# Moving the next unit's row preparation behind the output products in a linear-attention and mixture-of-experts kernel on one Trainium2 core

## The chip, the cores and the metric

The kernel runs on one core of a Trainium2 chip. The metric is the device time of one execution, in microseconds, and the value that counts is the median of several executions. A core has TensorE (in the profile PE for matmuls and PEld for loading the stationary operand), VectorE (DVE), ScalarE (ACT), GpSimd (POOL) and the queue engine SyncE (SP). The engines run side by side; each works through its own queue in order, and an instruction waits on semaphores for what other engines and the DMA transfers have done.

## What is computed

```python
x = A_x                                       # 2048 rows of 512
h = x + _A_ref(_layernorm(x), wqkv, w_phi, wo)  # linear attention, 32 heads
h2 = h + _B_ref(_layernorm(h), w_gate, w1, w2)  # 8 experts, one per row
# inside _B_ref, D=512, F=1792, E=8:
logits = xf @ w_gate
topk_idx = jnp.argsort(-logits, axis=-1)[:, :1]
for e in range(E):
    out = out + w * (_silu(xf @ w1[e]) @ w2[e])   # w: the gate where row picks e, else 0
```

All of it is in float32.

## The kernel before, in words

**Two parts.** The first part, up to about 300 us, computes the attention, writes h with its normalisation factors and gate into the buffer `hbuf` in device memory, and sorts the rows by their expert. The second part runs the experts, and the change is in it. Its rows are worked off in units of 128 rows, `unit(u)`. Here units 0 to 10 run first, then two wide stages of 288 rows (`wide(0)`, `wide(1)`), then units 11 and 12; later units are skipped by a test on the chip. `POS` is 11, so `POS - 1` is unit 10, which also prepares the wide stage.

**Products in two halves.** A float32 product is made of three fast ones: each operand is split into a high part (ACT writes it, `hi_of`, L76) and a low part (DVE subtracts, `lo_of`, L79), and `mm3` adds high x high, high x low and low x high (L82 to L84). The weights of an expert come in seven chunks of 1 MB (`raw`), each split in two pieces of 128x1024 into `whi` and `wlo`. Chunks 0, 1, 2 and the first half of chunk 3 hold the first weight matrix; the second half of chunk 3 holds the weights of output products 0 and 1, chunk 4 those of products 2 to 5, chunk 5 of 6 to 9, chunk 6 of 10 to 13.

**One unit.** `gather(u + 1)` fetches the rows of the next unit with an indirect DMA on POOL (`rows`, L145) into one of two row buffers `xg`; it must wait until the scatter of unit u - 1 has read that buffer. `gemm1` makes the hidden values in four column chunks (PSUM tile `mh`), ACT applies silu (L183, tile `hs`), PE transposes each chunk (`tr`, L209, PSUM tile `mtr`), and ACT and DVE split the transposed values (`hA` for chunks 0 and 1, `hThi` and `hTlo` for 2 and 3; the last one is half as wide, 128x256). `g2` makes fourteen output products into PSUM tile `my`, three matmuls each. DVE scales them by the gate and adds h (before: L1077), and POOL scatters the rows to the output (`scatter`, L152).

**Preparing the next rows.** `prework(u + 1)` normalises the gathered rows (ACT L161 for units 1 and 2, DVE L163 after that; tile `xn`), lets PE transpose them (L166, four transposes into another `mtr` bank), and splits the result into `xhi` and `xlo`, which the next unit's `gemm1` reads. The trace shows some of these tiles under other names that share their memory (`xwh`, `xwl`). The `mtr` and `mh` tiles share four PSUM banks in turn. In unit 10, `tile0` does the same for the three tiles of the wide stage's 288 rows (DVE L893, PE L897).

**Splitting the next expert's weights.** `split(u, c)` (L884) does its work only if a flag computed on the chip says that unit u begins with another expert; `fetch` (L880, L881) then reloads `raw[c]` on SP. In this data units 4 to 7 and unit 9 are full of such splits.

**What sets the order.** The code is written in one sequence, and a scheduler puts each engine's instructions in an order of its own: what is ready first by its reckoning goes first, with the sequence of the code as priority. `after(i)` adds an order edge: what the block issues on i's engine stands behind i in that engine's queue, without a wait for its end. The order is fixed when the program is built, and an instruction that waits holds up all that stands behind it on its engine.

In the code before, `prework(u + 1)` stands ahead of the output products:

```python
load_flags(u + 1)
if u != POS:
    with after(si if u < 3 else None):
        prework(u + 1)
g2(py, 0, 2)
tr(3)
```

Of the kernel before, what the change touches and what calls it, by code (L numbers as in the profile page):

```python
# [15 lines left out]
OP = mybir.AluOpType  # L16
# [6 lines left out]
S, D, H, DH = 2048, 512, 32, 16  # L23
F, E = 1792, 8
NJ = 14
# [6 lines left out]
POS = 11  # L32
# [3 lines left out]
WC = 24  # L36
# [12 lines left out]
def kernel(  # L49
# [28 lines left out]
    def lo_of(dst, src, hi):  # L78
        return V.tensor_tensor(dst, src, hi.bitcast(F32), op=OP.subtract)  # L79
# [64 lines left out]
    def rows(dst, col, n=P):  # L144
        G.indirect_dma_start(out=dst[0:n, :], out_offset=None, in_=hbuf if col else hbuf[0:S // 2, :],  # L145
                             in_offset=bass.IndirectOffsetOnAxis(ap=gidx[0:n, col:col + 1], axis=0))
# [4 lines left out]
    def scatter(src, col, n=P):  # L151
        G.indirect_dma_start(out=out, out_offset=bass.IndirectOffsetOnAxis(ap=sidx[0:n, col:col + 1], axis=0),  # L152
                             in_=src[0:n, 0:D], in_offset=None, bounds_check=S - 1, oob_is_err=False)
# [4 lines left out]
    def prework(u, pool=None):  # L158
        g = xg[u % 2]
        if u < 3:  # L160
            A.activation(xn2[0][:, 0:D], g[:, 0:D], AF.Identity, bias=g[:, D:D + 1], scale=g[:, D + 1:D + 2])  # L161
        else:
            V.tensor_scalar(xn2[0][:, 0:D], g[:, 0:D], g[:, D + 1:D + 2], g[:, D:D + 1], op0=OP.mult, op1=OP.add)  # L163
        pt = pool.tile([P, 512], F32, name="mtx", tag="s") if pool else bank("mtr")
        for k in range(KD):
            T.transpose(pt[:, k * P:(k + 1) * P], xn2[0][:, k * P:(k + 1) * P], ident)  # L166
        ptv = pt.rearrange("p (k t) -> p k t", k=KD)
        h = hi_of(xhi[par(u)], ptv)
        return h, lo_of(xlo[par(u)], ptv, xhi[par(u)])

    pin = {}
# [28 lines left out]
    def split_chunk(c):  # L200
        for i in range(2):
            hi_piece(c, i)
            lo_piece(c, i)

    def tr(c, hTf=None):
        fw = FC[c]
        pt = bank("mtr")
        for j in range(fw // P):
            T.transpose(pt[:, j * P:(j + 1) * P], hs[c % 2][:, j * P:(j + 1) * P], ident)  # L209
        ptv = pt[:, 0:fw].rearrange("p (k t) -> p k t", t=P)  # L210
        n = JF - 4 * c if hTf is not None else fw // P
        if n > 0:
            hi_of(hThi[c][:, 0:n, :], ptv[:, 0:n, :])
            lo_of(hTlo[c][:, 0:n, :], ptv[:, 0:n, :], hThi[c][:, 0:n, :])
        if hTf is not None:
            n = max(n, 0)
            return hi_of(hTf[:, 4 * c + n - JF:4 * c + fw // P - JF, :], ptv[:, n:, :])
# [25 lines left out]
    def after(i):  # L243
        return tc.issue_after(i.ins) if i is not None else ExitStack()
# [638 lines left out]
    def split(u, c):  # L883
        with tc.If(flags[u][0] > 0):  # L884
            split_chunk(c)
        fetch(u, c)

    def load(c, e):
        nc.sync.dma_start(raw[c], w12_at(e, c))
# [10 lines left out]
    def tile0(t, src):  # L900
        o, n = WT[t]
        ptv = tile3(t, src, None)
        hi_of(xW[0][:, :, o:o + n], ptv)
        return lo_of(xW[1][:, :, o:o + n], ptv, xW[0][:, :, o:o + n])
# [44 lines left out]
    def wide_out(w, t, r):  # L949
# [4 lines left out]
        V.scalar_tensor_tensor(r[0:n, 0:D], pt[0:n, :], r[0:n, D + 2:D + 3], r[0:n, 0:D], op0=OP.mult, op1=OP.add)  # L954
        scatter(r, WC + 3 * w + t, n)

    def unit(u):
        def g2(py, j0, j1):
            for j in range(j0, j1):
                c, jj = divmod(j, 4)  # L960
                m = mm3(py, hThi[c][:, jj, :], hTlo[c][:, jj, :], w2_at(whi, j), w2_at(wlo, j),
                        j == 0, j == NJ - 1)
            return m

        def g2p(py, w, j0, j1):
            for j in range(j0, j1):
                c, jj = divmod(j, 4)
                m = T.matmul(py, hThi[c][:, jj, :], w2_at(w, j), start=w is whi and j == 0,
                             stop=w is wlo and j == JF - 1)
                if w is whi:  # L970
                    m = T.matmul(py, hTlo[c][:, jj, :], w2_at(w, j), start=False, stop=False)
            return m

        if u:
            if u == POS - 1:
                rows(xg[0], WC + 1)
                rows(xg[1], WC)
            elif u + 1 < NU and u != POS:
                gather(u + 1)
            for c in range(4):  # L980
                si = silu(c, gemm1(u, c))
                if c:
                    tr(c - 1)
                if u == 1 and c == 0:
                    with after(pin["g1"]), after(pin["y"]):
                        wide_rows()
                if u == POS:
                    if c < 2:
                        if c == 0:
                            split_chunk(3)  # L990
                            fetch(u, 3)
                            wide_out(1, 0, xr[0])
                            gather(u + 1)
                        wide_out(1, c + 1, xr[c + 1])
                        if c:
                            load(6, e11)
                elif c < 3:
                    split(u, 4 + c)
        else:
            tr(2, hTf())  # L1000
            h3 = tr(3, hTf())
        py = pss.tile([P, 512], F32, name="my", tag="s")
        if u == 0:
            with after(g2p(py, whi, 0, 2)):
                gm, sidx_ = index(scratch, lambda: g2p(py, whi, 2, 4))
            with after(gm):
                gm = g2p(py, whi, 4, JF)
            def plain(j0, j1):
                for j in range(j0, j1):
                    m = T.matmul(py, hTf()[:, j - JF, :], w2_at(raw, j), start=False, stop=False)  # L1010
                return m

            with after(gm):
                m = plain(JF, NJ)
            with after(sidx_), after(m):
                last, ft, fc = flags_of(scratch)
            with after(last), after(ft):
                lo_piece(3, 1)
                lo4 = split_lo(4)
                m = g2p(py, wlo, 0, 2)  # L1020
            with after(h3), after(lo4), after(m):
                xh, xl = prework(1)
            g2p(py, wlo, 2, JF)
            with after(xh), after(xl):
                load_fl(0, 8)
            load_flags(0)
            load_flags(1)
            ew0, ew1 = [nc.values_load(ewi[0:1, i:i + 1], engines=[ENG.SP], min_val=0, max_val=E - 1)
                        for i in range(2)]
            e11_ = nc.values_load(flg[96:97, POS:POS + 1], engines=[ENG.SP], min_val=0, max_val=E - 1)  # L1030
            we.extend((ew0, ew1, e11_))
            for c in range(4):
                fetch(0, c)
                split(1, c)
            with after(xh), after(xl):
                for c in (5, 6):
                    split_hi(c)
                    split_lo(c)
            V.tensor_copy(utot, endx[:, EV:EV + 1])
            for c in range(4, NW):  # L1040
                fetch(0, c)
        elif u == POS - 1:
            tile0(1, xg[0])
            rows(xg[0], WC + 2)
            tile0(0, xg[1])
            rows(xg[1], u)
            g2(py, 0, 2)
            tr(3)
            for c in range(4):
                split_chunk(c)  # L1050
                load(c, we[1])
            with after(g2(py, 2, 9)):
                tile0(2, xg[0])
            g2(py, 9, NJ)
        else:
            if u + 1 < NU:
                if u == 5:
                    load_fl(8, POS)
                if u == POS:
                    load_fl(NF, NU)  # L1060
                load_flags(u + 1)
                if u != POS:
                    with after(si if u < 3 else None):
                        prework(u + 1)
            g2(py, 0, 2)
            tr(3)
            if u == POS:
                prework(u + 1)
                split_chunk(6)
                fetch(u, 6)  # L1070
            if u + 1 < NU:
                for c in range(4):
                    split(u + 1, c)
            g2(py, 2, NJ)
        g = xg[u % 2 if u != POS - 1 else 1]
        with after(xl if u == 0 else None):
            pin["y"] = V.scalar_tensor_tensor(g[:, 0:D], py, g[:, D + 2:D + 3], g[:, 0:D], op0=OP.mult, op1=OP.add)  # L1077
        scatter(g, u)

    we = []  # L1080
    for u in range(POS):
# [94 lines left out]
```

## Time and profile before

| | |
|---|---|
| median of 3 runs | 744.52 us (741.51 to 744.82) |
| the profiled execution's own time | 743.65 us |
| its span, first to last instruction | 742.0 us |
| PE busy | 681.6 us (92%) |
| DVE busy | 475.3 us (64%) |
| ACT busy | 356.1 us (48%) |
| POOL busy | 186.6 us (25%) |
| mean granted TensorE clock | 0.965 |

The profile is one execution seen by the hardware profiler. The page gives the busy time of each engine and the costliest groups of instructions. The trace behind it answers finer questions: the table of stretches gives the busy time of each engine between two moments; the waits list who waited for whom; the timeline of an engine lists its instructions with start, length, engine, line, what is written from what, how many, and in square brackets the idle time before and what ended it. PE is near its full load over the whole span, so what matters are the stretches in which it is not.

### The profile page before, as it was taken

The numbers are of one execution on the slowest core, as the hardware profiler recorded it, in microseconds if no ns is written. First come the engines' busy times: TensorE is split into PE (matmuls) and PEld (weight loads), VectorE is DVE, ScalarE is ACT, GpSimd is POOL, SyncE is SP. The second block draws the span as 40 slices with busy tenths as digits, with TensorE's granted clock in tenths as the row PEclk, the third lists the DMA queues.
The fourth block names the chain that finished last, engine by engine and source line by source line (L and its number), as shares of the span: only waits on it lengthen the run. The fifth ranks groups of instructions, "written<-read, shape, count | busy, mean of one in ns | idle before, by whom it ended". The sixth has DMA issues, their size and how long they took to land. (4 is left out here: it accounts for less than half of the span.)

```text
span 742.0 us, 12255 instructions
## 1 busy us (share of the span) xinstructions
PE 681.6 (92%) x4231; PEld 605.6 (82%) x4231; DVE 475.3 (64%) x904; ACT 356.1 (48%) x570; POOL 186.6 (25%) x270
## 2 busy tenths in 40 slices
PE   9999999999999999986999977978985999999694
PEld 8998999899999998665887866866874899999583
DVE  5997888787785779750125876873395665376650
ACT  4453444433334367340225856852474565555640
POOL 2334553433334445200011101101112220240110
PEclk9999999999999999998999989999997999999897
DMA  9111110000013296182003957964286735644220
GB/s 336 49 30 30 43 30 15 28 15 1 1 30 96 78 342 256 43 310 118 30 30 141 350 208 291 345 223 161 97 311 249 246 103 187 226 173 171 100 86 18
DMA packets 24301, 103.77 MB, mean 140 GB/s; under 512 B 3294, under 2 KB 3806, under 8 KB 15264
## 3 DMA queue, kind: packets, MB, share of 16 engines
q1 hardware_dynamic: 20352, 91.01, 33.8%
q0 software_dynamic: 3584, 11.32, 4.5%
q8 instruction: 35, 0.57, 0.3%
q10 hardware_dynamic: 288, 0.52, 0.2%
q14 instruction: 42, 0.34, 0.1%
HBM read 94.43 MB, written 8.81 MB: 139 GB/s over the span
## 5 line engine op out<-in xcount | busy, mean ns | idle before, releaser
L79 DVE TENSOR_TENSOR wlo<-raw,whi 128x1024 fp32r<-128x1024 f32 (+1 forms) x147 | 168.7, 1170 | 30.9 <-ACT whi L76 25.1
L76 ACT ACTIVATE whi<-raw 128x1024 fp32r<-128x1024 f32 (+1 forms) x148 | 147.6, 1011 | 64.8 <-PE mh L84 27.2
L152 POOL DMA_INDIRECT out_dram<-xg,sidx x15 | 21.8, 1456 | 269.2 <-DVE xg L1077 142.4
L552 POOL TENSOR_TENSOR ph<-t,sm 128x1024 f32<-128x1024 f32 x32 | 62.1, 1939 | 94.0 <-DVE sm L550 58.8
L183 ACT ACTIVATE hs<-mh 128x512 f32<-128x512 f32 (+1 forms) x52 | 28.0, 538 | 51.3 <-PE mh L84 50.3
L209 PE MATMUL mtr<-ident,hs 128*128 128x128 f32 x182 | 30.7, 288 | 21.4 <-DVE hA L79 17.6
L544 ACT ACTIVATE t<-t 128x1024 f32<-128x1024 f32 x32 | 33.9, 1060 | 27.2 <-DVE t L543 22.9
L209 PEld LDWEIGHTS mtr<-ident,hs 128*128 128x128 f32 x182 | 23.4, 148 | 28.7 <-issue 20.9
L145 POOL DMA_INDIRECT xg<-hbuf,gidx x23 | 26.8, 1163 | 79.3 <-DMA out_dram<-xg,sidx 43.5
L163 DVE TENSOR_SCALAR xn<-xg 128x512 f32<-128x512 f32 x11 | 6.0, 546 | 61.9 <-DMA xg<-hbuf,gidx 49.9
L549 DVE TENSOR_REDUCE sm<-t 128x64 f32<-128x1024 f32 x32 | 38.8, 1215 | 10.4 <-ACT t L544 10.2
L82 PE MATMUL my<-whi,hA 128*128 128x512 f32 x96 | 44.1, 459 | 0.0
L82 PE MATMUL mh<-whi,xhi 128*128 128x512 f32 (+1 forms) x112 | 42.4, 379 | 0.0
L83 PE MATMUL mh<-wlo,xhi 128*128 128x512 f32 (+1 forms) x112 | 41.3, 368 | 0.0
L84 PE MATMUL mh<-whi,xlo 128*128 128x512 f32 (+1 forms) x112 | 41.2, 368 | 0.0
L83 PE MATMUL my<-wlo,hA 128*128 128x512 f32 x96 | 41.1, 428 | 0.0
L84 PE MATMUL my<-whi,hA 128*128 128x512 f32 x96 | 41.0, 427 | 0.0
L82 PE MATMUL po<-wohi,xh 128*128 128x260 f32 x128 | 37.5, 293 | 0.9 <-DVE lg L679 0.9
L82 PE MATMUL mh<-whi,xwh 128*128 128x512 f32 (+1 forms) x96 | 36.1, 376 | 0.7 <-ACTq L884 0.7
L83 PE MATMUL po<-wolo,xh 128*128 128x260 f32 x128 | 36.3, 283 | 0.0
L83 PE MATMUL pv<-wvlo,xh 128*128 128x260 f32 x128 | 36.2, 283 | 0.0
L1077 DVE SCALAR_TENSOR_TENSOR xg<-my,xg 128x512 f32<-128x512 f32 x13 | 9.7, 748 | 41.3 <-PE my L84 41.3
(322 smaller groups left out, 2017.4 us busy)
## 6 DMA issues: line engine op xcount, KB each, us to landing
raw<-in_w_dram SPq DMA_DIRECT2D x70, 1024.0 KB, 5.6
xt<-in_x_dram SPq DMA_DIRECT2D x30, 256.0 KB, 2.6
hbuf<-hb SPq DMA_DIRECT2D x8, 515.0 KB, 3.6
phT<-in_wqkT_dram SPq DMA_DIRECT2D x4, 512.0 KB, 7.6
phT<-in_wv_dram SPq DMA_DIRECT2D x2, 512.0 KB, 7.5
phT<-in_wo_dram SPq DMA_DIRECT2D x2, 512.0 KB
phT<-in_woT_dram SPq DMA_DIRECT2D x2, 512.0 KB, 10.1
xt<-in_x_dram ACTq DMA_DIRECT2D x2, 256.0 KB
```

Source lines behind the costliest of these rows:

```text
L76: return A.activation(dst, src, AF.Copy)
L79: return V.tensor_tensor(dst, src, hi.bitcast(F32), op=OP.subtract)
L82: T.matmul(ps, ahi, bhi, start=first, stop=False)
L83: T.matmul(ps, ahi, blo, start=False, stop=False)
L84: return T.matmul(ps, alo, bhi, start=False, stop=last)
L145: G.indirect_dma_start(out=dst[0:n, :], out_offset=None, in_=hbuf if col else hbuf[0:S // 2, :], in_offset=bass.IndirectOffsetOnAxis(ap=gi ...
L152: G.indirect_dma_start(out=out, out_offset=bass.IndirectOffsetOnAxis(ap=sidx[0:n, col:col + 1], axis=0), in_=src[0:n, 0:D], in_offset=None ...
L183: return A.activation(hs[c % 2][:, 0:fw], p[:, 0:fw], AF.Silu)
L209: T.transpose(pt[:, j * P:(j + 1) * P], hs[c % 2][:, j * P:(j + 1) * P], ident)
L544: A.activation(t, t, AF.Exp)
L549: V.tensor_reduce(sm, t, AX.X, OP.add)
L552: G.tensor_tensor(ph.rearrange("p (a f) -> p a f", f=DH), t, bc(sm, DH), op=OP.mult)
```

## The change

The change keeps every computation and moves where some of it stands.

- In units 1 to 9, 11 and 12, `prework(u + 1)` stands behind the fifth output product (in unit 11 behind the eighth): PE's transposes behind that product, the DVE work behind the low part of the last hidden transpose (`pin["lo"]`). The splits of the next unit's chunks 0 and 1 are written ahead of it, those of chunks 2 and 3 behind it.
- In unit 10, `tile0` for the three wide tiles stands behind the 4th, 6th and 12th product, with the row gathers and the weight loads between them.
- The result of unit 0 is written ahead of the last splits of chunks 5 and 6, whose low parts are put behind it; before, they could stand ahead of it.
- The tables for the wide stage (`wide_rows`, in unit 1) are written one chunk later.

```diff
--- before.py
+++ after.py
@@ -211,7 +211,7 @@
         n = JF - 4 * c if hTf is not None else fw // P
         if n > 0:
             hi_of(hThi[c][:, 0:n, :], ptv[:, 0:n, :])
-            lo_of(hTlo[c][:, 0:n, :], ptv[:, 0:n, :], hThi[c][:, 0:n, :])
+            pin["lo"] = lo_of(hTlo[c][:, 0:n, :], ptv[:, 0:n, :], hThi[c][:, 0:n, :])
         if hTf is not None:
             n = max(n, 0)
             return hi_of(hTf[:, 4 * c + n - JF:4 * c + fw // P - JF, :], ptv[:, n:, :])
@@ -954,6 +954,10 @@
         V.scalar_tensor_tensor(r[0:n, 0:D], pt[0:n, :], r[0:n, D + 2:D + 3], r[0:n, 0:D], op0=OP.mult, op1=OP.add)
         scatter(r, WC + 3 * w + t, n)
 
+    def result(u, py, g):
+        pin["y"] = V.scalar_tensor_tensor(g[:, 0:D], py, g[:, D + 2:D + 3], g[:, 0:D], op0=OP.mult, op1=OP.add)
+        scatter(g, u)
+
     def unit(u):
         def g2(py, j0, j1):
             for j in range(j0, j1):
@@ -981,7 +985,7 @@
                 si = silu(c, gemm1(u, c))
                 if c:
                     tr(c - 1)
-                if u == 1 and c == 0:
+                if u == 1 and c == 1:
                     with after(pin["g1"]), after(pin["y"]):
                         wide_rows()
                 if u == POS:
@@ -1032,7 +1036,8 @@
             for c in range(4):
                 fetch(0, c)
                 split(1, c)
-            with after(xh), after(xl):
+            result(0, py, xg[0])
+            with after(xh), after(pin["y"]):
                 for c in (5, 6):
                     split_hi(c)
                     split_lo(c)
@@ -1040,18 +1045,23 @@
             for c in range(4, NW):
                 fetch(0, c)
         elif u == POS - 1:
-            tile0(1, xg[0])
-            rows(xg[0], WC + 2)
-            tile0(0, xg[1])
-            rows(xg[1], u)
             g2(py, 0, 2)
             tr(3)
-            for c in range(4):
+            with after(g2(py, 2, 4)), after(pin["lo"]):
+                tile0(1, xg[0])
+            rows(xg[0], WC + 2)
+            for c in range(2):
                 split_chunk(c)
                 load(c, we[1])
-            with after(g2(py, 2, 9)):
+            with after(g2(py, 4, 6)):
+                x0 = tile0(0, xg[1])
+            rows(xg[1], u)
+            for c in range(2, 4):
+                split_chunk(c)
+                load(c, we[1])
+            with after(g2(py, 6, 12)), after(x0):
                 tile0(2, xg[0])
-            g2(py, 9, NJ)
+            g2(py, 12, NJ)
         else:
             if u + 1 < NU:
                 if u == 5:
@@ -1059,23 +1069,24 @@
                 if u == POS:
                     load_fl(NF, NU)
                 load_flags(u + 1)
-                if u != POS:
-                    with after(si if u < 3 else None):
-                        prework(u + 1)
             g2(py, 0, 2)
             tr(3)
             if u == POS:
-                prework(u + 1)
                 split_chunk(6)
                 fetch(u, 6)
             if u + 1 < NU:
-                for c in range(4):
+                jp = 8 if u == POS else 5
+                for c in range(2):
                     split(u + 1, c)
-            g2(py, 2, NJ)
-        g = xg[u % 2 if u != POS - 1 else 1]
-        with after(xl if u == 0 else None):
-            pin["y"] = V.scalar_tensor_tensor(g[:, 0:D], py, g[:, D + 2:D + 3], g[:, 0:D], op0=OP.mult, op1=OP.add)
-        scatter(g, u)
+                with after(g2(py, 2, jp)), after(pin["lo"]), after(si if u < 3 else None):
+                    prework(u + 1)
+                for c in range(2, 4):
+                    split(u + 1, c)
+                g2(py, jp, NJ)
+            else:
+                g2(py, 2, NJ)
+        if u:
+            result(u, py, xg[u % 2 if u != POS - 1 else 1])
 
     we = []
     for u in range(POS):
```

## The prediction

> **What bounds the kernel now.** First I read the span of the page and then the table of stretches with one row for each unit, from the unit's first matmul to that of the next. Columns: the stretch and its length, busy time and count of PE, PEld, DVE, ACT and POOL, the granted TensorE clock, the DMA share, GB/s.
>
> ```profile
> span 742.0 us, 12255 instructions
> 317.49:350.40 32.91, 23.86 (x111) 19.63 (x112) 10.81 (x30) 8.40 (x13) 2.03 (x2) 0.90 0.62 241
> 350.40:371.80 21.40, 21.40 (x110) 17.93 (x109) 4.30 (x7) 4.62 (x9) 1.99 (x2) 1.00 0.08 26
> 393.09:416.75 23.66, 21.78 (x109) 17.86 (x108) 18.11 (x20) 17.39 (x22) 2.91 (x2) 1.00 0.59 214
> 416.75:445.06 28.31, 23.78 (x110) 19.81 (x109) 20.64 (x22) 18.73 (x23) 2.72 (x2) 0.88 0.73 277
> 445.06:472.39 27.33, 23.14 (x109) 19.13 (x108) 20.54 (x22) 18.68 (x23) 2.72 (x2) 0.94 0.77 293
> 472.39:500.41 28.02, 23.12 (x110) 19.29 (x108) 20.64 (x22) 18.68 (x23) 2.72 (x2) 0.94 0.75 279
> 500.41:527.11 26.70, 23.17 (x109) 19.13 (x108) 6.69 (x9) 5.80 (x10) 1.99 (x2) 0.94 0.32 118
> 527.11:550.86 23.75, 21.68 (x109) 17.81 (x108) 17.84 (x20) 17.41 (x22) 4.81 (x4) 1.00 0.62 223
> 550.86:583.90 33.04, 25.19 (x118) 20.46 (x117) 22.48 (x25) 19.32 (x25) 7.62 (x4) 0.85 0.76 278
> 678.92:709.72 30.80, 24.85 (x122) 20.64 (x121) 17.41 (x20) 18.78 (x24) 4.58 (x4) 0.89 0.34 121
> ```
>
> The rows are units 1, 2, 4 to 10 and 11. Unit 2 is PE from end to end: 21.40 us, the floor of a unit. Units 4 to 7 and 9 also split an expert's weights, about 18 to 21 us of DVE, which still fits under 21.4. What the others have over 21.4 is PE standing still, or the half clock that follows: 0.94 over 27.33 us is 0.06 x 27.33 x 2 = 3.3 us at half clock, which costs 1.6.
>
> Next the waits from 300 us on: one row of the view of all engines, then PE's own. Columns: who waited for whom, us in total, times, longest.
>
> ```profile
> DVE xn L163 <- DMA xg<-hbuf,gidx: 49.9, 9, 9.9
> ```
>
> ```profile
> PE mtr L209 <- DVE hA L79: 17.6, 7, 4.9
> PE mtr L166 <- ACT xn L161: 8.4, 1, 8.4
> PE mtr L897 <- DVE xn L893: 7.9, 1, 7.9
> PE mtr L166 <- issue: 6.0, 1, 6.0
> ```
>
> PE's transposes of the hidden rows (L209) wait for DVE, and DVE waits for the gathered rows of the next unit. Unit 6 shows how, in the timelines of DVE and POOL:
>
> ```profile
> 447.49 0.74 DVE L1077 SCALAR_TENSOR_TENSOR xg<-my,xg 128x512 f32<-128x512 f32 x1
> 448.15 3.66 DVE L79 TENSOR_TENSOR wlo<-raw,whi 128x1024 fp32r<-128x1024 f32 x3
> ...
> 458.83 0.55 DVE L163 TENSOR_SCALAR xn<-xg 128x512 f32<-128x512 f32 x1 [5.64 <-DMA xg<-hbuf,gidx]
> 459.29 0.68 DVE L79 TENSOR_TENSOR hA<-mtr,hA 128x512 fp32r<-128x512 f32 x1
> 459.89 2.35 DVE L79 TENSOR_TENSOR wlo<-raw,whi 128x1024 fp32r<-128x1024 f32 x2
> ...
> 462.76 0.68 DVE L79 TENSOR_TENSOR hTlo<-mtr,hThi 128x512 fp32r<-128x512 f32 x1
> ...
> 463.96 2.35 DVE L79 TENSOR_TENSOR wlo<-raw,whi 128x1024 fp32r<-128x1024 f32 x2
> 466.23 0.42 DVE L79 TENSOR_TENSOR hTlo<-mtr,hThi 128x256 fp32r<-128x256 f32 x1
> ```
>
> ```profile
> 448.51 1.74 POOL L152 DMA_INDIRECT out_dram<-xg,sidx  x1 [22.48 <-DVE xg L1077]
> 453.30 0.98 POOL L145 DMA_INDIRECT xg<-hbuf,gidx  x1 [3.05 <-DMA out_dram<-xg,sidx]
> ```
>
> The result of unit 5 (L1077) frees its row buffer by a scatter, the gather for unit 7 goes into that buffer, and the rows are there 458.83 - 447.49 = 11.34 us after the result began. The normalisation L163 stands in DVE's queue ahead of the low part of the first hidden transpose (hA), so DVE idles 5.64 us, and the bank that PE's third transpose needs is not freed.
>
> **The change, unit by unit.** Unit 2 shows the places on PE:
>
> ```profile
> 361.12 0.60 PE L209 MATMUL mtr<-ident,hs 128*128 128x128 f32 x4
> 361.56 0.60 PE L166 MATMUL mtr<-ident,xn 128*128 128x128 f32 x4
> 361.92 0.47 PE L82 MATMUL my<-whi,hA 128*128 128x512 f32 x1
> 371.80 0.40 PE L82 MATMUL mh<-whi,xwh 128*128 128x512 f32 x1
> ```
>
> The third transpose starts 361.12 - 350.40 = 10.72 us into the unit. Fourteen output products and a half-size transpose take 371.80 - 361.92 = 9.88, so a product (three matmuls) is about 0.69. In the new order the fifth product ends at 10.72 + 0.44 + 5 x 0.69 + 0.2 = 14.8 us, the next unit's row transposes stand there, and nine products (6.2) follow.
>
> Units 5, 6, 7. Nothing is removed; L163 (0.55) goes behind the last low part (hTlo, 128x256), and so DVE no longer blocks. What is late next is DVE itself. From the result, at +2.43 us in unit 6 (447.49 - 445.06), the queue up to that low part holds the result (0.67), eight weight pieces of chunks 0 to 3 (2.35 / 2 = 1.18 each, 9.4), three low parts of 0.6 and one of 0.4: 2.43 + 12.3 = 14.7, with L163 15.3 us. The rows land at +13.8, before that. ACT adds to it: the second half of chunk 3 also holds the weights of the first two products, so its high part starts after they end, at 10.72 + 0.44 + 1.4 = 12.6 us, and ACT has other parts in between:
>
> ```profile
> 402.15 1.06 ACT L76 ACTIVATE whi<-raw 128x1024 fp32r<-128x1024 f32 x1 [0.26 <-PE mh L84]
> 403.59 0.59 ACT L76 ACTIVATE hA<-mtr 128x512 fp32r<-128x512 f32 x1
> ```
>
> In unit 4 (start 393.09) the last hidden high part before the stall ends at 404.18, +11.1. I add the fourth activation (0.3), the third transpose's high part (0.5) and the two high pieces of chunk 3 (1.0 each), by which it is 13.9; then DVE's last weight piece (1.2), the low part (0.4) and L163 (0.55): 16.1. That is 1.3 us behind the fifth product, my value, by the order that unit 6 shows (pieces of chunk 3 ahead of the last low part). With those two pieces behind L163 it is before 14.8 and costs nothing. L163 can't slip further: the second half of chunk 4 holds the sixth product's weights, which PE uses only behind the row transposes, so chunks 4 to 6 stay behind L163. A wait of 1.3 us leaves the clock up: units 4 and 9 have about 2 us of idle time and 1.00. So 21.4 + 1.3 = 22.7 us each: 28.31, 27.33 and 28.02 become 22.7, a gain of 15.6. Queued behind L163 are the pieces of chunks 4 to 6, which PE needs only in the next unit's products, and the next rows' low part, due at 21.4.
>
> Units 4 and 9: the same places, 23.66 and 23.75 to 22.7, gain 2.0. Unit 8 splits nothing, so DVE is at L163 when the rows come; at unit 6's landing, 13.8 + 0.55 = 14.4, PE doesn't wait: 26.70 to 21.4, gain 5.3. Unit 2 has no wait to lose, nor have units 3 and 12: nothing.
>
> Unit 1. Here the rows themselves are late, since the first result stands behind the late pieces of chunks 5 and 6:
>
> ```profile
> 315.56 1.18 PE L968 MATMUL my<-wlo,hA 128*128 128x512 f32 x4
> 324.72 0.74 DVE L1077 SCALAR_TENSOR_TENSOR xg<-my,xg 128x512 f32<-128x512 f32 x1
> 325.75 1.04 POOL L152 DMA_INDIRECT out_dram<-xg,sidx  x1 [17.21 <-DVEq L884]
> 333.85 0.99 POOL L145 DMA_INDIRECT xg<-hbuf,gidx  x1 [7.07 <-DMA out_dram<-xg,sidx]
> 340.27 0.81 ACT L161 ACTIVATE xn<-xg 128x512 f32<-128x512 f32 x1 [9.68 <-DMA xg<-hbuf,gidx]
> ```
>
> The product of unit 0 ends at 316.7, so the result can run at about 317 to 319.5 and everything after it comes 5 to 7 us earlier: with the scatter 1.0 behind the result's start, rows at 332.5 to 335 with the same transfer times (325.75 to 340.27, 14.5), at 328 to 331 with unit 6's 10.3 (448.51 to 458.83). The fifth product ends at 317.49 + 14.8 + about 0.7 for the wide tables' transposes, 333.0. Between these I take 332 for the rows; with 0.81 on ACT, PE waits some 0.4: 21.4 + 0.7 + 0.4 = 22.5, gain 10.4, bounds 7 (half clock again) and 11. The four pieces that now stand behind the result are pushed by 0.74 us; chunk 6 is due at the eleventh product, some 337.
>
> Unit 10. The rows of the first wide tile come late by the scatter that runs beside the weight loads:
>
> ```profile
> 554.79 4.02 POOL L152 DMA_INDIRECT out_dram<-xg,sidx  x1 [10.34 <-DVE xg L1077]
> 566.08 0.98 POOL L145 DMA_INDIRECT xg<-hbuf,gidx  x1 [7.27 <-DMA out_dram<-xg,sidx]
> ```
>
> ```profile
> 571.63 1.12 PE L897 MATMUL mtr<-ident,xn 128*128 128x128 f32 x4 [7.85 <-DVE xn L893]
> ```
>
> Scatter to gather took 11.3 us here, 4.8 in unit 6. PE's wait of 7.9, which ends at 571.63 - 550.86 = +20.8, began behind two products; now it begins behind six, and eight products and two transposes remain: 20.8 + 6.3 + 2 for the half clock that a wait of 5 us brings (0.85 in this unit's row) = 29.1, gain 4.0, bounds 0 and 10. The gathers that follow on POOL (third wide tile, the unit's own rows again) stand behind the moved normalisations and are due at the twelfth product and at the result; SP's loads keep their order. In the other units the moved step issues no DMA. The Trainium skill, page "DMA: Bandwidth & Descriptors", section "Queues, rings and completion order", says that each DMA engine takes turns between queues packet by packet, by which 256 KB of rows would not wait 11 us beside loads; the measured 11.3 against 4.8 speaks against it, and by the page the unit would take near 23 us.
>
> Unit 11: the wait of 6.0 us (a scatter still reading the tile that L163 writes) began behind two products and now begins behind eight, 6 x 0.69 = 4.1 later, and a wait of 1.9 us leaves the clock up (units 4 and 9): 0.11 x 30.80 x 2 = 6.8 us at half clock go, of which I take 4 to have been work, worth 2. Gain 4.1 + 2 = 6, bounds 4 and 8.
>
> Sum: 15.6 + 2.0 + 5.3 + 10.4 + 4.0 + 6.0 = 43.3. The profiled execution took 743.65 us, 0.9 under the median of 744.52 and inside its runs: 743.65 - 43.3 = 700.3 us.
>
> **Rivals.** (a) The rows land later, because POOL's issues and the transfers now meet a DVE and a DMA that don't pause. For it: the issue took 4.02 and 1.74 us where weight pieces ran, 0.98 where DVE was idle. 4.02 for 0.98 puts the rows at +16.8, L163's end at 17.4: 1.3 more in each of units 4 to 7 and 9, 2.6 in unit 8, near 9 us in all, 709. Against it: the share of DMA was only 0.77. The Trainium skill, page "SBUF — State Buffer", section "SBUF: two separate sides", says that DVE and GpSimd take a shared port pair as an exclusive lock, DVE with two SBUF inputs too; the row of 4.02 us agrees, that of 1.74 less.
>
> (b) Chunk 3's pieces come behind L163, and unit 10's rows come as in unit 6: 5 x 1.3 + 6 = 12.5 less, 688.
>
> (c) Slower. L163 late holds chunks 4 to 6 behind it, these hold the result, and the result starts the next rows: a loop of landing + 0.55 + about 8 us (low part, six pieces, their high parts). At 11.34 it is under 22.7. At 19 us from result to rows it is 27.6 plus 1.7 of half clock, 29.3 in each of units 4 to 9: 175.8 against 157.8, +18, which eats the gains of units 1 (there 6 left) and 11: 750. It decides from about 18 us; the worst seen is unit 10's, from 1.0 before its scatter (as in unit 6) to 0.6 before 571.63, 17.2.
>
> (d) The scheduler leaves the order as it is: 743.7. Against it: each new place is an order edge on that engine.
>
> **Numbers.** Forecast 0.62, (a) 0.17, (b) 0.12, (c) 0.06, (d) 0.03. The range goes from (b) to a little over (a), 687 to 714, and leaves out (c), (d) and the tails. Within 0.5% (3.7 us), about what a measurement of this kernel can tell from no change, is (d) alone: faster 0.91, same 0.03, slower 0.06.
>
> **What would show it.** Right: no DVE idle time before hA for L163; L163 behind hTlo of 128x256; PE's only waits in units 4 to 7 near the sixth product, 1 to 2 us, clock 1.00; the first result before 320 us and no wait of PE at 341; unit 10 still waiting for L893, unit 11 under 2.5 us. Wrong: waits of over 4 us at L166, or results drifting more than 3 us behind a unit's end.

## The result and the profile after

| | before | after |
|---|---|---|
| median of 4 runs | 744.63 us (741.51 to 744.82) | 707.52 us (705.88 to 711.28) |
| ratio | | 0.9518, 95% interval 0.9473 to 0.9563 |
| the profiled execution | 743.65 us | 707.62 us |
| mean granted TensorE clock | 0.965 | 0.985 |

The forecast was 700.3 us, in a range of 687 to 714. The change made the kernel faster, as forecast, and the time lies in the range; the forecast was 7.3 us too low against the profiled execution.

First the table of stretches of the changed kernel, one row for each unit, columns as in the table of before: units 1, 2, 4 to 11.

```profile
318.92:344.19 25.27, 22.19 (x112) 18.20 (x113) 10.86 (x30) 8.29 (x13) 3.07 (x2) 1.00 0.81 313
344.19:365.61 21.42, 21.42 (x109) 17.88 (x108) 4.40 (x7) 4.73 (x9) 1.99 (x2) 1.00 0.09 26
...
386.93:409.79 22.86, 21.63 (x110) 17.80 (x109) 18.23 (x19) 17.16 (x22) 2.92 (x2) 1.00 0.60 215
409.79:432.61 22.82, 21.55 (x110) 17.77 (x109) 20.47 (x22) 18.26 (x23) 3.52 (x2) 1.00 0.88 341
432.61:459.96 27.35, 23.18 (x109) 18.97 (x108) 21.04 (x23) 18.34 (x23) 2.72 (x2) 0.94 0.81 310
459.96:482.75 22.79, 21.56 (x110) 17.77 (x109) 20.35 (x21) 18.22 (x23) 2.71 (x2) 1.00 0.87 315
482.75:504.83 22.08, 21.63 (x109) 17.80 (x108) 6.91 (x10) 5.80 (x10) 1.99 (x2) 1.00 0.42 160
504.83:527.61 22.78, 21.55 (x110) 17.77 (x109) 18.23 (x19) 17.16 (x22) 3.88 (x3) 1.00 0.64 228
527.61:554.31 26.70, 23.85 (x118) 19.32 (x116) 22.24 (x26) 19.25 (x25) 10.02 (x5) 0.95 0.90 346
649.32:674.00 24.68, 22.93 (x122) 19.03 (x121) 17.68 (x20) 17.51 (x24) 5.08 (x4) 1.00 0.36 120
```

Units 4, 5, 7 and 9 stand at 22.8 us with the clock at 1.00, as forecast. Unit 6 stands out: 27.35 us, exactly what it took before, with the clock at 0.94. Units 1 and 10 also have time above the rest.

Then PE's waits from 300 us on (who waited for whom, us in total, times, longest).

```profile
PE mtr L166 <- DVE xn L163: 9.6, 6, 4.2
PE mtr L897 <- DVE xn L893: 2.9, 1, 2.9
PE mtr L166 <- ACT xn L161: 2.4, 1, 2.4
PE mtr L166 <- issue: 1.8, 1, 1.8
```

The 17.6 us of waits at the hidden transposes (L209) are gone. What remains is at the moved row transposes (L166): one of 4.2 us and five that share the other 5.4.

Unit 6 again, timeline of DVE and of POOL:

```profile
435.04 0.74 DVE L958 SCALAR_TENSOR_TENSOR xg<-my,xg 128x512 f32<-128x512 f32 x1
435.70 3.66 DVE L79 TENSOR_TENSOR wlo<-raw,whi 128x1024 fp32r<-128x1024 f32 x3
...
440.66 0.68 DVE L79 TENSOR_TENSOR hA<-mtr,hA 128x512 fp32r<-128x512 f32 x1
...
447.82 0.41 DVE L79 TENSOR_TENSOR hTlo<-mtr,hThi 128x256 fp32r<-128x256 f32 x1
451.07 0.55 DVE L163 TENSOR_SCALAR xn<-xg 128x512 f32<-128x512 f32 x1 [2.83 <-DMA xg<-hbuf,gidx]
```

```profile
436.07 1.74 POOL L152 DMA_INDIRECT out_dram<-xg,sidx  x1 [15.43 <-DVE xg L958]
444.07 0.98 POOL L145 DMA_INDIRECT xg<-hbuf,gidx  x1 [6.27 <-DMA out_dram<-xg,sidx]
```

The order is the one that was predicted: hA no longer waits, and L163 is behind the last low part. But scatter to gather took 444.07 - 436.07 = 8.0 us, where the same unit took 4.8 before, and the rows were there 451.07 - 432.61 = 18.5 us into the unit, not 13.8. DVE idled 2.83 us and PE 4.2.

Unit 1, timelines of DVE, POOL and ACT:

```profile
317.91 0.69 DVE L79 TENSOR_TENSOR xwl<-mtr,xwh 128x512 fp32r<-128x512 f32 x1 [1.35 <-ACT xwh L76]
320.84 0.75 DVE L958 SCALAR_TENSOR_TENSOR xg<-my,xg 128x512 f32<-128x512 f32 x1 [2.24 <-DVEq L884]
```

```profile
321.87 2.08 POOL L152 DMA_INDIRECT out_dram<-xg,sidx  x1 [11.90 <-DVEq L884]
329.55 0.99 POOL L145 DMA_INDIRECT xg<-hbuf,gidx  x1 [5.60 <-DMA out_dram<-xg,sidx]
```

```profile
336.65 0.81 ACT L161 ACTIVATE xn<-xg 128x512 f32<-128x512 f32 x1 [5.37 <-DMA xg<-hbuf,gidx]
```

The result still stands behind 2.24 us in which DVE's queue waits at the test of a flag (L884), the rows come at 336.65 instead of the forecast's 332, and PE waits 2.4.

### The profile page after: what moved, and what is told of

Read it like the earlier page. It is cut to its first block, busy times and chain, and to the rows that moved or that the text cites. A ratio compares the mean times of both kernels' runs of the same rounds, so it can differ in the third digit from the quotient of the medians.

```text
span 705.9 us, 12252 instructions
## 1 busy us (share of the span) xinstructions
PE 672.8 (95%) x4231; PEld 597.2 (85%) x4231; DVE 476.5 (67%) x904; ACT 354.2 (50%) x570; POOL 190.1 (27%) x270
## 5 line engine op out<-in xcount | busy, mean ns | idle before, releaser
L79 DVE TENSOR_TENSOR wlo<-raw,whi 128x1024 fp32r<-128x1024 f32 (+1 forms) x147 | 167.8, 1170 | 28.2 <-ACT whi L76 25.6
L76 ACT ACTIVATE whi<-raw 128x1024 fp32r<-128x1024 f32 (+1 forms) x148 | 145.8, 1009 | 54.2 <-PE mh L84 25.3
L145 POOL DMA_INDIRECT xg<-hbuf,gidx x23 | 30.8, 1341 | 82.4 <-DMA out_dram<-xg,sidx 44.2
L544 ACT ACTIVATE t<-t 128x1024 f32<-128x1024 f32 x32 | 33.9, 1060 | 27.2 <-DVE t L543 22.9
L549 DVE TENSOR_REDUCE sm<-t 128x64 f32<-128x1024 f32 x32 | 38.8, 1214 | 10.4 <-ACT t L544 10.2
L82 PE MATMUL my<-whi,hA 128*128 128x512 f32 x96 | 41.0, 427 | 0.0
L84 PE MATMUL my<-whi,hA 128*128 128x512 f32 x96 | 38.4, 400 | 0.0
L83 PE MATMUL my<-wlo,hA 128*128 128x512 f32 x96 | 38.2, 398 | 0.0
L84 PE MATMUL pv<-wvhi,xl 128*128 128x260 f32 x128 | 36.2, 283 | 0.0
L82 PE MATMUL pv<-wvhi,xh 128*128 128x260 f32 x128 | 36.1, 282 | 0.0
L84 PE MATMUL po<-wohi,xl 128*128 128x260 f32 x128 | 36.1, 282 | 0.0
L79 DVE TENSOR_TENSOR hA<-mtr,hA 128x512 fp32r<-128x512 f32 (+1 forms) x26 | 17.6, 676 | 26.6 <-ACTq L884 16.2
```

What stands on the lines that cost most here:

```text
L76: return A.activation(dst, src, AF.Copy)
L82: T.matmul(ps, ahi, bhi, start=first, stop=False)
L83: T.matmul(ps, ahi, blo, start=False, stop=False)
L84: return T.matmul(ps, alo, bhi, start=False, stop=last)
L544: A.activation(t, t, AF.Exp)
L549: V.tensor_reduce(sm, t, AX.X, OP.add)
```

## The experiments

The first theory: DVE's queue, blocked by a normalisation that waits for rows, cost units 4 to 9 their time; the early result gave unit 1, the later transposes units 10 and 11; what is left in units 6 and 1 comes from rows that land late beside the reloads of the weights. Rivals: the gain comes from PE's own order; or the rows are late because POOL's issues and DVE share a port.

Each ratio below compares a kernel with runs of the kernel before taken alongside it; the medians of these lay between 741.23 and 744.63 us, so the medians of two experiments compare to some 3 us only.

For each profiled execution, the length of a unit in us, from the start of its first matmul to that of the next (unit 10 to the first matmul of the wide stage):

| kernel | 1 | 4 | 5 | 6 | 7 | 8 | 9 | 10 | 11 | median us |
|---|---|---|---|---|---|---|---|---|---|---|
| before | 32.9 | 23.7 | 28.3 | 27.3 | 28.0 | 26.7 | 23.8 | 33.0 | 30.8 | 744.63 |
| after | 25.3 | 22.9 | 22.8 | 27.4 | 22.8 | 22.1 | 22.8 | 26.7 | 24.7 | 707.52 |
| result alone | 30.8 | 23.7 | 27.5 | 27.5 | 27.6 | 26.5 | 23.8 | 33.0 | 30.8 | 739.61 |
| rows alone | 32.2 | 22.9 | 22.8 | 27.5 | 22.8 | 21.4 | 22.8 | 31.9 | 30.2 | 724.69 |
| no DVE edge | 27.1 | 23.2 | 30.1 | 31.1 | 28.6 | 27.2 | 23.3 | 24.3 | 28.2 | 735.68 |
| 7th product | 24.0 | 21.5 | 21.4 | 21.5 | 21.4 | 21.4 | 21.4 | 24.2 | 24.9 | 691.78 |
| quarter loads | 22.6 | 22.9 | 22.8 | 22.9 | 22.8 | 21.4 | 22.8 | 23.8 | 24.5 | 696.80 |
| early result | 22.6 | 22.9 | 23.6 | 27.6 | 22.8 | 21.4 | 22.8 | 24.9 | 24.6 | 703.46 |
| 7th and early | 22.6 | 21.5 | 21.4 | 21.5 | 21.4 | 21.4 | 21.4 | 26.9 | 24.7 | 692.46 |
| 9th and early | 22.6 | 21.5 | 29.5 | 21.4 | 21.3 | 21.4 | 21.3 | 27.3 | 24.5 | 700.19 |
| 7th in 5 | 25.4 | 22.9 | 21.4 | 28.2 | 22.8 | 21.4 | 22.8 | 24.3 | 24.7 | 705.19 |
| 7th in 6 | 25.3 | 22.9 | 22.8 | 26.2 | 22.8 | 21.4 | 22.8 | 24.4 | 24.7 | 704.48 |
| 7th in 4, 5 | 27.9 | 21.5 | 21.5 | 22.9 | 28.2 | 21.4 | 22.8 | 25.1 | 24.6 | 699.06 |
| 7th in 5, 6 | 26.9 | 22.9 | 25.7 | 21.5 | 22.8 | 21.4 | 22.8 | 24.4 | 24.8 | 702.40 |

### The result's place alone

The kernel before, with the wide stage's tables one chunk later, as in the change, and

```diff
+            result(0, py, xg[0])
-            with after(xh), after(xl):
+            with after(xh), after(pin["y"]):
                 for c in (5, 6):
...
-        scatter(g, u)
+        if u:
+            result(u, py, xg[u % 2 if u != POS - 1 else 1])
```

> The kernel before with one edit alone: the first result is written ahead of the late splits (and the wide tables one chunk later). If the result's place is what made unit 1 long, unit 1 (32.91 us before, 25.27 after) falls by 7 to 8 us and all other units stay as before: about 736 us. If the move of the normalisation was needed in unit 1 too, because the rows still land behind the place where PE wants them early in the unit, unit 1 keeps a wait of several us at the row transposes and gains 3 to 5 us: about 740. If the rows of unit 1 are late whatever the result does, 743 to 744.

Measured: 739.61 us (734.29 to 744.80), ratio 0.9947 (0.9910 to 0.9984). PE's timeline in unit 1:

```profile
336.15 1.11 PE L166 MATMUL mtr<-ident,xn 128*128 128x128 f32 x4 [5.39 <-ACT xn L161]
```

The row transposes run 5 us sooner than the 341.14 of before, but behind two products PE still waits 5.39 us, and the half clock follows (0.89 over the unit). Unit 1 gained 2.2 us: the second case, and less than it gave.

### The moved rows alone

The kernel before, with `prework(u + 1)` moved in units 1 to 9 and 12 as in the change; the first result, unit 10 and unit 11 as before.

> The kernel before with the next unit's normalisation and transposes moved in units 1 to 9 and 12, the first result, unit 10 and unit 11 left as before. My theory: units 4, 5, 7, 8 and 9 come to 22 to 23 us as in the changed kernel, unit 6 stays near 27, unit 1 gains only 0 to 3 us since its rows still start behind the late result, units 10 and 11 as before (33 and 31): about 725 us, 19 below. The rival, that the units hang together so that the move brings its gain only with the early result: units 4 to 9 keep waits of 3 to 5 us and the time is over 735.

Measured: 724.69 us (722.94 to 726.20), ratio 0.9755 (0.9706 to 0.9803), as the theory had it, unit by unit. Units 10 and 11, whose code stood as before, took 31.9 and 30.2 us, so what they gained in the change is due to the edits in them. Unit 1 gained 0.7 us: PE waited 7.7 us at the transposes. So in unit 1 the two parts are worth 2.2 and 0.7 us alone and 7.6 together: either alone leaves PE a wait of over 5 us and the half clock.

### Without the edge on DVE

```diff
-                with after(g2(py, 2, jp)), after(pin["lo"]), after(si if u < 3 else None):
+                with after(g2(py, 2, jp)), after(si if u < 3 else None):
```

> The changed kernel without the order edge on DVE (the normalisation isn't held behind the last low part; PE's edge behind the fifth product stays). My theory (DVE's queue, blocked by a normalisation that waits for rows, cost units 4 to 9 their time): the normalisation goes back ahead of the hidden low parts, PE waits for those again, units 5 to 7 come back to 26 to 28 us and the time to 720 to 726. The rival (PE's own order, the transposes behind the fifth product, brings the gain): no change, 705 to 710.

Measured: 735.68 us (731.97 to 738.66), ratio 0.9909 (0.9877 to 0.9941): 28 us of the change's gain are gone. DVE's timeline in unit 6:

```profile
456.93 0.55 DVE L163 TENSOR_SCALAR xn<-xg 128x512 f32<-128x512 f32 x1 [8.52 <-DMA xg<-hbuf,gidx]
457.39 0.68 DVE L79 TENSOR_TENSOR hA<-mtr,hA 128x512 fp32r<-128x512 f32 x1
```

```profile
PE mtr L209 <- DVE hA L79: 22.1, 5, 7.1
```

The normalisation is back ahead of hA, and PE waits at L209 for 22.1 us, more than the 17.6 of before. In unit 6 PE's row transposes stood behind the fifth product as in the change, so PE's order alone isn't what brings the gain. The time is beyond what was expected, since these rows come late too (DVE idled 8.52 us, 5.64 before), and here the whole delay stands ahead of hA.

### Transposes behind the seventh product

```diff
-                jp = 8 if u == POS else 5
+                jp = 8 if u == POS else 7
```

> The changed kernel with the next unit's transposes behind the seventh product in place of the fifth, 1.4 us later. My theory: PE's waits at the row transposes (1.4 to 1.6 us in units 4, 5, 7 and 9, 2.4 in unit 1, 4.2 in unit 6) shrink by 1.4 us each and with them the half clock behind the longer ones: 697 to 700 us. The rival: what is late moves on by as much, since pieces of chunk 4 now go ahead of the normalisation on DVE, or since the next unit's first matmul then waits for the low part of its rows: 706 to 709, with waits at the start of the units in place of those in the middle.

Measured: 691.78 us (691.27 to 693.55), ratio 0.9311 (0.9277 to 0.9346), below the theory's 697 to 700. From 341 to 513 us PE has no wait at all. Unit 6, the timelines of POOL and DVE and the row of the stretches:

```profile
430.63 1.74 POOL L152 DMA_INDIRECT out_dram<-xg,sidx  x1 [15.42 <-DVE xg L958]
435.61 0.98 POOL L145 DMA_INDIRECT xg<-hbuf,gidx  x1 [3.23 <-DMA out_dram<-xg,sidx]
```

```profile
442.73 0.54 DVE L163 TENSOR_SCALAR xn<-xg 128x512 f32<-128x512 f32 x1
```

```profile
427.18:448.68 21.50, 21.50 (x109) 17.81 (x108) 20.54 (x22) 18.58 (x23) 2.72 (x2) 1.00 0.97 372
```

Here the rows of unit 6 came in time: 4.98 us from scatter to gather, no idle time ahead of L163. A place 1.4 us later took away 4.2 us of wait, which the theory of rows that land at a fixed late time can't give. The DMA share was 0.97, higher than in the changed kernel (0.81 over a longer unit), so its mean load alone doesn't make rows late. What differs is how long the reloads issued in unit 6 take to land (how many, size of one, median us from issue to landing), first in the changed kernel, then here:

```profile
raw<-in_w_dram SPq DMA_DIRECT2D x6, 1024.0 KB, 7.5
```

```profile
raw<-in_w_dram SPq DMA_DIRECT2D x8, 1024.0 KB, 5.0
```

### A quarter of the loads

```diff
-            nc.sync.dma_start(raw[c], w12_at(nx_, c))
+            nc.sync.dma_start(raw[c][:, 0:CW // 4], w12_at(nx_, c)[:, 0:CW // 4])
```

> The changed kernel, reloading only a quarter of each chunk of an expert's weights in the units (three quarters of these loads' bytes are left out, so the products there use old weights; every split and product is still done). If the loads beside them make the rows late: scatter to gather takes 4 to 6 us in place of 7 to 8 in units 1, 6 and 8, unit 6 comes to 22.8 us, unit 1 to 22.5 to 23.5, unit 8 to 21.4: about 698 us. If POOL's and DVE's sharing of a port makes the rows late, the splits are the same and so are these units: 705 to 710.

Measured: 696.80 us in one run, beside 741.23 for the kernel before. Unit 6, POOL and the row of the stretches:

```profile
433.53 1.74 POOL L152 DMA_INDIRECT out_dram<-xg,sidx  x1 [17.14 <-DVE xg L958]
438.31 0.98 POOL L145 DMA_INDIRECT xg<-hbuf,gidx  x1 [3.04 <-DMA out_dram<-xg,sidx]
```

```profile
430.07:452.93 22.86, 21.66 (x109) 17.80 (x108) 20.47 (x22) 18.23 (x23) 2.72 (x2) 1.00 0.36 102
```

The splits are all there (DVE 20.47 us), POOL's issues took the same 1.74 and 0.98 us, and the DMA moved 102 GB/s instead of 310: scatter to gather is 4.78 us, unit 6 is 22.86, unit 1 22.6 and unit 8 21.4. Unit 6 alone would not show the cause, since with the seventh product it was in time with all the bytes. Unit 8 does: POOL there in the changed kernel, then here.

```profile
486.21 1.01 POOL L152 DMA_INDIRECT out_dram<-xg,sidx  x1 [16.59 <-DVEq L884]
493.63 0.97 POOL L145 DMA_INDIRECT xg<-hbuf,gidx  x1 [6.41 <-DMA out_dram<-xg,sidx]
```

```profile
479.18 1.01 POOL L152 DMA_INDIRECT out_dram<-xg,sidx  x1 [17.12 <-DVEq L884]
482.33 0.97 POOL L145 DMA_INDIRECT xg<-hbuf,gidx  x1 [2.14 <-DMA out_dram<-xg,sidx]
```

Scatter to gather took 3.15 us instead of 7.42, with the same issues; it was 5.9 to 7.4 in the profile of every kernel that reloads whole chunks, and unit 1's fell from 7.7 to 5.5. So the bytes of the reloads make the rows late, not POOL's port. The 1.4 us waits of units 4 to 7 and 9 stay, since those are DVE's queue.

### The first result ahead of the flags

```diff
+            result(0, py, xg[0])
-            with after(xh), after(xl):
+            with after(xh), after(pin["y"]):
                 load_fl(0, 8)
...
-            result(0, py, xg[0])
```

> The changed kernel with the first result written ahead of the loading of the flags as well. If DVE's 2.2 us of idle time for the flags, ahead of the first result, make unit 1's rows late: the result comes 2 to 3 us earlier (near 318 us) and unit 1's wait at the row transposes (2.4 us) goes, 25.27 to 22 to 23 us: 704 to 705 us. If the transfers beside them decide when the rows land, no change in unit 1: 707.

Measured: 703.46 us (702.67 to 705.72), ratio 0.9501 (0.9453 to 0.9550). Timelines of DVE and POOL:

```profile
316.74 0.74 DVE L958 SCALAR_TENSOR_TENSOR xg<-my,xg 128x512 f32<-128x512 f32 x1
```

```profile
317.75 1.03 POOL L152 DMA_INDIRECT out_dram<-xg,sidx  x1 [9.56 <-DVEq L884]
323.45 0.99 POOL L145 DMA_INDIRECT xg<-hbuf,gidx  x1 [4.66 <-DMA out_dram<-xg,sidx]
```

The result ran where the forecast had put it, scatter to gather took 5.7 us instead of 7.7, and unit 1 has no wait at L166: 22.6 us. Its first matmul, though, now waits 1.7 us for ACT's queue at the test of a flag (L884), 0.7 in the changed kernel. The ratios of this kernel and the change overlap, so the gain in the total is not shown, that in unit 1 is.

### Both together, and two products later still

The early result with `jp` 7, and with `jp` 9.

> Both improvements together: transposes behind the seventh product (691.8 us alone) and the first result ahead of the flags (703.5 us alone, 4.1 below the changed kernel, 2.7 of it in unit 1). If they add up, unit 1 loses its last wait (24.04 to 21.8 to 22.6 us) and nothing else changes: 689 to 690.5 us. If not (the earlier result starts the loads of the weights otherwise, and later units wait for rows again, as unit 5 did in the run with the early result alone, 23.55 us): 692 to 696.

Measured: 692.46 us (691.59 to 693.21), ratio 0.9325 (0.9298 to 0.9353): the same as the seventh product alone. Unit 1 gave 1.5 us; it began 1.2 us later, at 318.68 against 317.44, and unit 10 took 26.9 us instead of 24.2.

> The first result ahead of the flags and the transposes behind the ninth product, two products (1.4 us) later still. If no wait is left at the seventh, this gains nothing (21.4 us is the floor of a unit), and the rows' high and low parts have 1.4 us less until the next unit's first matmul: the last transpose then ends some 3.9 us (5 products and a bit) ahead of the unit's end, against a high part of 0.6 and a low part of 0.7 and the pieces queued ahead of them, up to 1.2 to 2.4 on DVE: no change to 1 us a unit, 689 to 696.

Measured: 700.19 us (694.48 to 704.85), ratio 0.9428 (0.9384 to 0.9472), outside what was expected. Not the start of the next units, as feared, but unit 5's rows: POOL and DVE there.

```profile
408.79 5.15 POOL L152 DMA_INDIRECT out_dram<-xg,sidx  x1 [19.21 <-DVE xg L958]
420.35 0.98 POOL L145 DMA_INDIRECT xg<-hbuf,gidx  x1 [6.41 <-DMA out_dram<-xg,sidx]
```

```profile
408.43 4.63 DVE L79 TENSOR_TENSOR wlo<-raw,whi 128x1024 fp32r<-128x1024 f32 x4
```

The scatter's issue took 5.15 us, not 1.74, while four weight pieces ran on DVE without a gap, and the gather came 11.56 us behind it. The Trainium skill, page "SBUF — State Buffer", section "SBUF: two separate sides", says that GpSimd, which writes the descriptors of such a DMA, is locked out of the port pair that it shares with DVE while some kinds of DVE instructions run. This row agrees with that, and the 1.74 beside three pieces in unit 6 less. Why it happened here and not in the other kernels wasn't tried.

### Which unit pays

Four kernels with the later place in some units only: unit 5, unit 6, units 4 and 5 (the edit shown), units 5 and 6.

```diff
-                jp = 8 if u == POS else 5
+                jp = 8 if u == POS else 7 if u in (4, 5) else 5
```

> The changed kernel with the later place (behind the seventh product) in unit 5 alone. My theory of unit 6's 27.35 us: the wait in the middle of unit 5 holds DVE's weight pieces back, the reloads that they free come bunched behind it (issued at 431.07, 433.03 and 435.31 us in the changed kernel), and unit 6's scatter at 436.07 queues behind two or three of them. So without unit 5's wait unit 6 finds its rows on time: unit 5 21.4 us, unit 6 22.8, scatter to gather about 5 us; with the clock, 701 to 702. The rival (unit 6's rows are late by its own loads): unit 6 stays at 27, 705.5 to 707.

Measured: 705.19 us (702.70 to 708.43), ratio 0.9514 (0.9474 to 0.9554); unit 6 28.2 us, scatter to gather 7.58. Unit 6's rows were late without a wait in unit 5, so that wait is not the only cause.

> The counterpart: the later place in unit 6 alone. My theory: its rows still land 18.4 us into the unit, 16.2 is where the seventh product ends, so the wait falls from 4.2 to about 2.7 us and unit 6 from 27.35 to 25 to 26; scatter to gather stays near 8 us: 705 to 706.5. The rival (unit 6's own place decides when its rows come): unit 6 21.5 to 22, 701 to 702.

Measured: 704.48 us (702.49 to 706.72), ratio 0.9500 (0.9461 to 0.9539); unit 6 26.2 us, scatter to gather 7.99, as expected: its own place only hides 1.4 us of the same lateness.

> The changed kernel with the later place in units 4 and 5, unit 6 behind the fifth product as before. With the later place in unit 5 alone unit 6 stayed at 28.2 us, in unit 6 alone at 26.2, in all units it was 21.5. If a backlog of loads is built up over several units by the waits ahead of unit 6, and unit 4's is the other part of it: unit 6's scatter to gather takes 5 us and the unit 22.5 to 23.0; units 4 and 5 21.5; about 699 us. If unit 6's own place is needed for it (its transposes 1.4 us later meet rows that come no earlier): unit 6 stays at 27 to 28, about 703.

Measured: 699.06 us (697.25 to 706.67), ratio 0.9389 (0.9326 to 0.9452); the profiled execution is the one of 706.67, the slowest, and the other five took 697.25 to 703.77, so what follows need not hold for them. Unit 6 was in time, 22.9 us, as the theory of a backlog from earlier waits had it, but now unit 7, with nothing changed in it, was late. POOL and DVE in unit 7:

```profile
458.79 1.74 POOL L152 DMA_INDIRECT out_dram<-xg,sidx  x1 [17.00 <-DVE xg L958]
465.49 1.97 POOL L145 DMA_INDIRECT xg<-hbuf,gidx  x1 [4.97 <-DMA out_dram<-xg,sidx]
```

```profile
474.03 0.55 DVE L163 TENSOR_SCALAR xn<-xg 128x512 f32<-128x512 f32 x1 [3.17 <-DMA xg<-hbuf,gidx]
```

> The counterpart: the later place in units 5 and 6, unit 4 behind the fifth product. If the backlog comes from unit 4's wait as well: unit 6's scatter to gather stays over 7 us, its rows land near 18 and the unit takes 25.5 to 27: 702 to 704 us. If units 5 and 6 together are what it takes: unit 6 21.5, about 699 us.

Measured: 702.40 us (696.63 to 705.81), ratio 0.9441 (0.9357 to 0.9525). Unit 6 was in time (21.5), but unit 5 was late: 25.7 us, scatter to gather 411.77 to 419.40, 7.6 us.

So in each of these four profiles one unit of 5, 6 and 7 pays. A full DMA beside its scatter is not enough for it: with the seventh product in all units no unit pays, though the DMA share from 429.57 to 439.57 us, around unit 6's scatter and gather, is 1.00 to 1.01.

The traces say more when the bytes are counted. Take the bytes of the reloads issued from 380 us on, when none is outstanding, less those of their DMA packets begun by the end of the scatter's issue: what is left is the backlog that the scatter meets. In the 13 profiles with whole reloads, units 5 to 7 have 37 scatters whose issue took 1.74 us. With a backlog of 0.65 to 0.74 MB (23 of them) scatter to gather took 4.8 to 5.7 us; with 0.76 to 1.11 MB (14) it took 5.4 to 8.4, and the late units of the four kernels are all among these. Unit 6 met 0.65 MB in the kernel before, 1.11 in the change and 0.65 with the seventh product; with a quarter of the loads it met 0.26.

The larger backlogs go with reloads issued closer together ahead of the scatter, and most of these follow a unit in which PE waits 1.4 us behind the fifth product. Among the late units of the four kernels, unit 6 of the first (0.76 MB, 7.58 us) is the one that doesn't. No run changed the spacing of whole reloads by itself, so this is a pattern found in the traces, not a cause shown; and each row of the table is one profiled execution.

## Why the prediction was right, point by point

Sums against the two profiled executions, in us:

| part | forecast | measured |
|---|---|---|
| units 5, 6, 7 | 15.6 | 5.49 - 0.02 + 5.23 = 10.70 |
| units 4 and 9 | 2.0 | 0.80 + 0.97 = 1.77 |
| unit 8 | 5.3 | 4.62 |
| unit 1 | 10.4 | 7.64 |
| unit 10 | 4.0 | 6.34 |
| unit 11 | 6.0 | 6.12 |
| the rest | 0 | -1.16 |
| sum | 43.3 | 743.65 - 707.62 = 36.03 |

**Right.** That DVE's queue was the cause is shown by the kernel without its edge, where the waits at L209 come back. What is late next, DVE itself at the sixth product, was sized at 1.3 us; units 4, 5, 7 and 9 show 1.4 over the floor. Two products later the wait is gone and the units are at 21.4 to 21.5: it was the queue up to the last low part, as worked out. In units 4, 5, 7 and 9 DVE had no idle time for the rows ahead of L163. Unit 11's wait fell to 1.8 us (forecast 1.9) and its clock rose from 0.89 to 1.00. Two of the signs named ahead went the other way: the first result came at 320.84 us, not before 320, and unit 6's 4.2 us is a wait of over 4 us at L166, which was named as a sign of being wrong.

**The mis-sized term: "The rows land at +13.8, before that."** It took the landing in unit 6 from the trace of before as a fixed time. In the changed kernel the rows of that unit landed at +18.5, which cost 4.65 us; in units 5 and 7 they did not hold DVE up. The step had no term for the reloads that are still to be moved when the scatter is issued. Rival (a) had named this, "the transfers now meet a DVE and a DMA that don't pause", and put the time at 709, but priced it by POOL's issue; the issue took 1.74 us as before, and the quarter of the loads shows that it was the bytes. That the pause is missing doesn't suffice, though: with the seventh product unit 6 has less of it still (21.50 us), and its gather, issued at 435.61, landed 5.3 us later, at +13.7. The argument against the rival, a share of 0.77, was a mean over a unit and could not tell these cases apart.

**Unit 1, "the result can run at about 317 to 319.5".** It ran at 320.84. Unit 0's product had itself ended 1.4 us later than before, at 318.2, and against that the result is inside what was forecast, at its late end: the loading of the flags, 2.24 us of DVE's idle time, stands ahead of it. The term that was mis-sized is the transfer, for which the step took a value between the shorter time and the longer; the longer held: 321.87 to 336.65 is 14.8 us, 14.5 before. With the result at 316.74 unit 1 took 22.6 us, where the forecast had 22.5.

**Unit 10, "20.8 + 6.3 + 2".** The rows came sooner than that: the scatter's issue took 1.74 us instead of 4.02, and scatter to gather 5.8 instead of 11.3 (POOL's timeline):

```profile
531.07 1.74 POOL L152 DMA_INDIRECT out_dram<-xg,sidx  x1 [9.02 <-DVE xg L958]
536.88 1.89 POOL L145 DMA_INDIRECT xg<-hbuf,gidx  x1 [4.07 <-DMA out_dram<-xg,sidx]
```

Rows nearly as in unit 6 were a condition of rival (b), not of the forecast; here they brought 2.3 us of its 6. In the sum they hide part of what units 1 and 6 fell short, which is luck. Across the kernels that have the new unit 10 it took 23.8 to 27.3 us.

**The rest.** Unit 1 began 1.43 us later than before, and unit 0's product had ended later by as much already; in the other kernels unit 1 began between 315.8 and 319.0. In the stretch from 50 to 100 us the granted clock was 0.93, and 0.97 before:

```profile
50.00:100.00 50.00, 50.00 (x321) 45.41 (x320) 40.05 (x68) 21.29 (x34) 24.30 (x38) 0.93 0.12 33
```

With the seventh product it was 0.97 again, so this looks like a difference between executions. Rival (c), a loop of late rows and late results, didn't come: in every kernel that keeps the edge, the unit behind one of over 25 us was back at 21.4 to 22.8 us.

## What to carry to other kernels

An instruction that waits for a transfer costs what stands behind it in its queue: put it behind the last thing that somebody else is waiting for, and give its consumer a place later than the end of that queue; here the seventh product instead of the fifth brought the ratio from 0.9518 to 0.9311, some 15 us. The landing time of a small transfer isn't a constant to be carried from one trace into another: in this kernel it went with the bytes of the large loads still to be moved when it was issued, so count those, and not the mean share. Two edits on the same wait don't add: price the wait that is left by either alone, with the half clock that it brings.

## What was not expected of the hardware

Unit 1 has the ten microseconds in which the DMA of the changed kernel moved most (last two columns: share, GB/s):

```profile
328.00:338.00 10.00, 6.92 (x45) 5.70 (x43) 2.83 (x20) 2.77 (x5) 0.99 (x1) 1.00 1.02 426
```

At a share of 1.02 the 16 DMA engines moved 426 GB/s; the Trainium skill, page "Perfetto Trace Analysis", section "Roofline", gives about 435 GB/s as what a single core's DMA engines can do, and this row agrees. Near that limit the time from a scatter to the gather behind it was not steady: 4.98 us in unit 6 with the seventh product, at a share of 0.97 over the unit, and 6.7 to 8.0 in the units that paid (11.6 in the one with the slow issue). A mean share doesn't tell which of the two it will be; the backlog at the scatter, 0.65 MB there and 0.76 to 1.11 MB in the late units with the usual issue, tells more.
